# Later selection work for four head pairs and an earlier start of one feed-forward block, in a fused attention and MLP kernel on one Trainium2 core

## The chip, the cores and the metric

The kernel runs on one core of one Trainium2 chip. The metric is the device time of one execution in microseconds (us), and a smaller time is better. Each timed comparison runs both kernels in the same rounds on the same chip. "Span" is the length of one profiled execution, from the first to the last instruction; it is about 1.7 us shorter than the time of the same execution.

The engines of the core have short names in the profile: PE is TensorE (matrix multiplications), PEld its weight loads, DVE is VectorE, ACT is ScalarE, POOL is GpSimd, and SP is the sync engine, which here only starts DMA transfers (SPq is its queue). "L388" is line 388 of the kernel.

## The reference, cut to what matters

The model is an attention in which each query may only look at its six best chunks of keys, followed by a gated MLP with a spatial mixing matrix. There are 4 batch rows, 8 heads, 768 positions and 64 dimensions per head.

```python
def _attn_ref(q, k, v):                       # q, k, v: (4, 8, 768, 64)
    k_chunks = k.reshape(B, H, nc, 32, D)
    k_min, k_max = k_chunks.min(axis=3), k_chunks.max(axis=3)
    ub = np.sum(np.maximum(q[..., None, :] * k_min[:, :, None], q[..., None, :] * k_max[:, :, None]), -1)
    ub = np.where(causal, ub, -1e9)           # an upper bound for each query and chunk
    top_chunks = np.argsort(ub, axis=-1)[..., -6:]
    scores = scale * q @ k.transpose(0, 1, 3, 2)
    scores = np.where(sel & causal_mask, scores, -1e9)     # sel: the key's chunk is in top_chunks
    ...                                        # softmax
    return attn @ v

def _moe_ref(x, w_in, w_spatial, b_spatial, w_out):
    u, v = np.split(np.maximum(x @ w_in, 0.0), 2, axis=-1)
    v_n = (v - mean(v)) / sqrt(var(v) + 1e-6)
    v_s = einsum('ts,bsd->btd', w_spatial, v_n) + b_spatial[None, :, None]
    return (u * v_s) @ w_out
```

## The kernel before

The kernel works on 16 pairs of heads, four pairs to a batch row. It has one list of "beats", 12 to a pair; every piece of work is put at a beat, and the pieces are emitted in the order of beats. A beat is therefore not a time. It sets the order in which the pieces are handed over when the program is built, and so in the main the order of each engine's queue; each engine takes its queue in that order.

For each pair, the selection comes first: transpose the keys (`k_transpose`), reduce them to maxima and minima of chunks (`k_max`, `k_min`, two DVE reductions), transpose the queries, build the bounds, find the sixth best bound (`top`, MAX8 instructions) and write the not-chosen marks beside the queries (`select`). Then the queries with their marks are transposed to the operand `a` of the score matmuls. Pairs 0 to 7 do this on TensorE with a copy on ACT; pairs 8 to 15 do it by one DMA transpose from the sync engine.

```python
ps_sc  = ...psum_pool(bufs=3)     # scores
ps_tr  = ...psum_pool(bufs=1)     # ONE bank: q_transpose, bounds and a_transpose (pairs 4 and up)
ps_acc = ...psum_pool(bufs=1)     # ONE bank: attention output of a head
ps_ml  = ...psum_pool(bufs=3)     # feed-forward, transposed keys, weight transposes (and transposes of pairs 0-3)
qs_ring = [ring.tile(...) for i in range(3)]          # queries: three buffers of two pairs each

def a_transpose(self, hi):                            # [cut]
    if self.i >= 8:
        if hi == 0:
            nc.sync.dma_start_transpose(out=self.a..., in_=self.qs...)      # L246
        return
    self.tr = self.trans_tile()
    for t in range(NQT):
        nc.tensor.transpose(self.tr[...], self.qs[:, t, ...], identity)     # L251

# [cut] the loads: queries on the POOL queue, L336, and values, L343
for g in range(1, NPAIR // 2):                        # g: two pairs
    t0 = 2 * g * BEATS
    for hi in range(2):
        at(t0 - 40 + hi, load_k, g, hi)
        at(t0 - 36 + hi, load_q, g, hi)
    at(t0 - 18, load_v, g)
# [cut] scores, exponentials and values of pair i at beats 12 i to 12 i + 17
for i, p in enumerate(pairs):                         # the selection of pair i
    t0 = i * BEATS
    if i < 2:
        continue
    t0 += 4 if i < 4 else 0
    at(t0 - (22 if i < 4 else 27), p.k_transpose)
    at(t0 - 22, p.k_max)
    at(t0 - 21, p.q_transpose)
    at(t0 - 20, p.k_min)
    at(t0 - 19, p.q_parts, 0)
    at(t0 - 18, p.q_parts, 1)
    at(t0 - 17, p.k_bounds)
    at(t0 - 16, p.bounds)
    at(t0 - 15, p.k_operand, 0)
    at(t0 - 14, p.top, 0)
    at(t0 - 13, p.top, 1)
    at(t0 - 12, p.select)
    at(t0 - 11, p.k_operand, 1)
    at(t0 - 10, p.a_transpose, 0)
    at(t0 - 9, p.a_copy, 0)
    at(t0 - 7, p.a_transpose, 1)
    at(t0 - 6, p.a_copy, 1)
# [cut] feed-forward of batch row b: its matmuls are spread evenly over a stretch of beats
    first, count = (b + 1) * HP * BEATS + 13, HP * BEATS      # HP = 4 pairs to a row
    for cost, fn in steps:
        at(first + done * count // total, fn)
```

The softmax here doesn't subtract the row's maximum and nothing guards it: scores larger than these inputs give would overflow.

## Time and profile before

The time before was 208.66 us (median of 3 runs, 208.53 to 208.81).

| quantity, before | value | from |
|---|---|---|
| span | 206.9 us | the page |
| columns streamed by TensorE, at 2400 per us (213 ns for 512) | 171.6 us | all matmul records, added up |
| DVE busy in all | 154.5 us | the page |
| first feed-forward matmul | 55.09 us | the timeline |
| first scores of pair 9 | 97.1 us | the timeline |

The first part of the page of the kernel before says how busy each engine was: busy us, share of the span, number of instructions.

```profile
PE 187.8 (91%) x1922; PEld 115.1 (56%) x1922; DVE 154.5 (75%) x454; ACT 158.1 (76%) x326; POOL 80.5 (39%) x100
```

TensorE looks full at 91%, but 206.9 us minus 171.6 us of streamed columns leaves about 35 us in which it streamed nothing (33 us at the measured pace below). The Trainium skill ("Perfetto Trace Analysis", section "Identifying the Most-Contended Engine") says that matmul busy share is not a good measure of how close a kernel is to the limit, and this trace agrees. The measured pace is close to the 213 ns: at the end of the chain of waits (start, duration, what), 146 matmuls of 512 columns take 31.53 us back to back, 216 ns each.

```profile
171.50 31.53 PE mlp L388 x146
```

The table of stretches shows where that time lies. Its columns are the stretch, its length, then busy us and number of instructions (in brackets) of PE, PEld, DVE, ACT and POOL, then the granted TensorE clock, the DMA share and GB/s.

```profile
26.00:40.00 14.00, 12.94 (x195) 9.87 (x194) 12.61 (x41) 12.18 (x26) 10.15 (x15) 1.00 2.07 171
40.00:55.00 15.00, 12.85 (x195) 9.68 (x194) 12.90 (x37) 14.26 (x32) 12.28 (x14) 1.00 1.82 172
55.00:80.00 25.00, 24.39 (x294) 16.17 (x292) 23.72 (x79) 22.38 (x48) 15.72 (x18) 1.00 2.03 136
80.00:97.10 17.10, 17.10 (x193) 10.80 (x192) 15.72 (x48) 12.80 (x28) 6.48 (x7) 1.00 1.57 137
97.10:160.00 62.90, 62.90 (x629) 37.04 (x628) 50.25 (x150) 55.10 (x121) 12.17 (x14) 1.00 0.92 140
```

From 80 to 160 us TensorE is busy in every moment. From 26 to 55 us it isn't, while DVE is busy for 25.5 of 29 us and ACT for 26.4. That is the stretch that the change is about. The timeline of DVE before (start, duration, engine, line, operation, output<-input, count) shows how tightly the selection stands there: the two key reductions of pair 4 (L178, L182) stand around a part of the MAX8 instructions (L232) and ahead of the select (L237) of pair 3.

```profile
33.23 0.94 DVE L178 TENSOR_REDUCE kmm<-kTp 128x24 f16<-128x768 f16 x1
34.09 0.44 DVE L232 MAX8 max<-ub 128x8 f32<-128x20 f32 x4
34.45 0.94 DVE L182 TENSOR_REDUCE kmm<-kTp 128x24 f16<-128x768 f16 x1
35.30 0.40 DVE L237 TENSOR_TENSOR qs<-ub,max 128x240 f16<-128x240 f32 x1
```

And the timeline of all engines before, where pair 4 gets its first transposed operand:

```profile
41.31 0.40 DVE L237 TENSOR_TENSOR qs<-ub,max 128x240 f16<-128x240 f32 x1
...
42.20 0.50 PE L251 MATMUL tr<-identity,qs 128*128 128x128 f16 x6
...
42.98 0.82 ACT L257 COPY a<-tr 128x768 f16<-128x768 f16 x1
```

The select at 41.31 is pair 4's; 0.9 us later TensorE transposes for the operand `a` (L251), and ACT copies it at 42.98. In the timeline of ACT before, from 47.3 us on, stand pair 4's first exponentials:

```profile
47.12 1.39 ACT L271 ACTIVATE e<-sc 128x512 f16<-128x512 f32 x2
```

They began more than 3 us after this copy ended, so pair 4's selection had slack.

### The profile page before, as it was taken

To read this page: it belongs to the slowest core of one execution; us is meant where nothing else is said; L and a number is where in the kernel's file an instruction comes from. 1 tells how busy PE (TensorE), PEld (TensorE's weight loads), DVE (VectorE), ACT (ScalarE), POOL (GpSimd) and SP (SyncE) were. 2 spreads that over 40 slices of the span, in tenths; PEclk is the share of its full clock that TensorE was granted. 3 is DMA by queue.
4 is the path that set the end of the run, shared out by engine and by line. 5 is a ranking of instruction groups with operands and counts; after the bars stand their busy time and mean duration, and the time that the engine had idled before them with its cause. 6 is when DMAs were issued, how large, how long until landed. Compare 5 with 4: busy or idle time off the path is not lost.

```text
span 206.9 us, 5068 instructions
## 1 busy us (share of the span) xinstructions
PE 187.8 (91%) x1922; PEld 115.1 (56%) x1922; DVE 154.5 (75%) x454; ACT 158.1 (76%) x326; POOL 80.5 (39%) x100
## 2 busy tenths in 40 slices
PE   0368999898899999999999999999999999999992
PEld 0266776775666665656655656565555454444440
DVE  6467979989799989899797999887647456365520
ACT  4797989899998889785989996669999830666042
POOL 7997659596992463236114111111111110000000
PEclk9999999999999999999999999999999999999999
DMA  5999999999999999979998926648782124540356
GB/s 38 92 118 154 140 178 158 173 177 167 177 162 162 97 119 128 135 130 147 149 278 153 180 62 57 127 88 158 181 166 65 38 29 92 187 152 3 72 128 256
DMA packets 114424, 27.27 MB, mean 132 GB/s; under 512 B 109536, under 2 KB 110816, under 8 KB 114400
## 3 DMA queue, kind: packets, MB, share of 16 engines
q0 software_dynamic: 76544, 12.20, 89.8%
q1 hardware_dynamic: 37856, 14.75, 36.4%
q8 instruction: 15, 0.25, 0.5%
q14 instruction: 9, 0.07, 0.1%
HBM read 24.38 MB, written 6.29 MB: 148 GB/s over the span
## 4 chain that ended last, share of the span: by engine, by line
PE 69%; ACT 17%; DVE 8%; issue 2%; DMA 2%; POOL 0%; DVEq 0%; ACTq 0%; POOLq 0%
PE mlp L388 40%; PE sc L266 12%; ACT e L271 10%; PE acc L289 7%; PE kTp L170 2%; ACT a L257 2%; DVE kmm L178 2%; PE ub L222 2%; DMA k<-in_k_dram 2%; PE trm L251 2%; ACT vraw L398 1%; PE tr L205 1%; DVE vn L412 1%; DVE kmm L182 1%; ACT u L420 1%
## 5 line engine op out<-in xcount | busy, mean ns | idle before, releaser
L271 ACT ACTIVATE e<-sc 128x512 f16<-128x512 f32 x192 | 96.9, 553 | 14.8 <-PE sc L266 13.4
L266 PE MATMUL sc<-a,kh 128*128 128x512 f16 (+3 forms) x256 | 65.5, 308 | 2.1 <-ACT e L271 1.5
L388 PE MATMUL mlp<-w_in_sb,xT 128*128 128x512 f16 x192 | 53.0, 379 | 0.1
L278 POOL TENSOR_SCALAR_AFFINE_SELECT e<-e 128x768 f16<-128x768 f16 x24 | 20.9, 869 | 66.3 <-ACT e L271 66.3
L289 PEld LDWEIGHTS <-e 128*128 128x128 f16 x672 | 31.4, 97 | 17.0 <-DVE x L297 3.8
L388 PE MATMUL mlp<-vn,wsT 128*128 128x512 f16 x144 | 37.3, 379 | 0.0
L289 PE MATMUL acc<-vt,e 128*128 128x65 f16 x672 | 35.3, 193 | 0.7 <-DVE x L297 0.4
L266 PEld LDWEIGHTS <-kh 128*128 128x128 f16 x256 | 22.7, 98 | 13.3 <-issue 0.8
L437 ACT COPY o<-mlp 128x512 f32<-128x512 f32 x24 | 14.1, 586 | 19.5 <-PE mlp L388 19.1
L400 DVE BATCH_NORM_STATS2 stats<-vraw 128x6 f32<-128x512 f32 x24 | 16.6, 693 | 12.9 <-ACT vraw L398 12.5
L388 PE MATMUL mlp<-w_out_sb,gT 128*128 128x512 f16 x96 | 25.1, 379 | 0.0
L388 PEld LDWEIGHTS <-xT 128*128 128x128 f16 x192 | 17.2, 97 | 12.6 <-issue 0.4
L427 DVE SCALAR_TENSOR_TENSOR g<-mlp,b_col,u 128x512 f16<-128x512 f32 x24 | 17.9, 748 | 7.3 <-PE mlp L388 6.2
L232 DVE MAX8 max<-ub 128x8 f32<-128x8 f32 (+4 forms) x160 | 15.6, 165 | 5.1 <-PE ub L222 4.9
L388 PEld LDWEIGHTS <-wsT 128*128 128x128 f16 x144 | 12.9, 98 | 10.4
L178 DVE TENSOR_REDUCE kmm<-kTp 128x24 f16<-128x768 f16 x16 | 15.2, 948 | 3.7 <-PE kTp L170 2.7
L297 DVE TENSOR_TENSOR x<-acc,rec 128x384 f16<-128x384 f32 x32 | 17.6, 551 | 0.4
L336 POOL DMA_DIRECT2D qs<-in_q_dram x14 | 14.6, 1049 | 5.9 <-PE sc L266 5.9
L194 DVE COPY kh<-kTp 64x768 f16<-64x768 f16 x30 | 16.5, 549 | 0.5
L398 ACT ACTIVATE vraw<-mlp 128x512 f32<-128x512 f32 x24 | 14.4, 601 | 3.0 <-PE mlp L388 3.0
L420 ACT ACTIVATE u<-mlp 128x512 f16<-128x512 f32 x24 | 14.3, 598 | 1.7 <-PE mlp L388 1.5
L327 POOL DMA_DIRECT2D k<-in_k_dram x14 | 14.4, 1045 | 2.5 <-PE kTp L170 1.8
(67 smaller groups left out, 230.2 us busy)
## 6 DMA issues: line engine op xcount, KB each, us to landing
out_dram<-o SPq DMA_DIRECT2D x24, 256.0 KB, 2.3
vt<-in_v_dram POOLq DMA_DIRECT2D x8, 384.0 KB, 8.8
k<-in_k_dram POOLq DMA_DIRECT2D x14, 192.0 KB, 8.1
qs<-in_q_dram POOLq DMA_DIRECT2D x14, 192.0 KB, 7.5
ws_raw<-in_moe_w_spatial_dram POOLq DMA_DIRECT2D x6, 192.0 KB, 6.9
w_in_sb<-in_moe_w_in_dram POOLq DMA_DIRECT2D x8, 128.0 KB, 6.9
w_out_sb<-in_moe_w_out_dram POOLq DMA_DIRECT2D x4, 128.0 KB, 7.9
k<-in_k_dram POOLq DMA_DIRECT2D x4, 96.0 KB, 3.4
```

The source lines that it names most:

```text
L178: nc.vector.tensor_reduce(self.kmm[:, 0, :], self.kT.rearrange("d (c ch) -> d c ch", ch=CHUNK), axis=AX.X, op=Alu.max)
L194: copy(self.kh[hi][d0:d1], self.kT[d0:d1])
L266: mm(sc[:, col:col + n], lhsT=self.kh[hi][:, t * P:(t + 1) * P], rhs=self.a[:, q0 // P:(q0 + n) // P, hi, :], start=True, stop=not diag)
L271: nc.scalar.activation(out=self.e[hi][:, g * 512:g * 512 + width], in_=sc[:, 0:width], func=Act.Exp, scale=scale)
L278: nc.gpsimd.affine_select(out=blk, in_=blk, compare_op=Alu.is_ge, fill=0.0, base=0, channel_multiplier=-1, pattern=[[0, NQT], [1, P]])
L289: mm(self.av[:, qi, :], lhsT=self.e[hi][:, c:c + P], rhs=self.v[hi][:, t, 0:D + 1], start=first and n == 0, stop=last and n == len(blocks) ...
L297: nc.vector.tensor_tensor(self.x16[:, :, hi, :], in0=self.av[:, :, 0:D], in1=rec.to_broadcast([P, NQT, D]), op=Alu.mult)
L388: mm(st[group][:, 0:cols], lhsT=lhsT, rhs=rhs, start=(j == 0), stop=(j == n - 1))
L398: nc.scalar.activation(st["vraw"][:, ti, :], h, func=Act.Relu)
L400: nc.vector.bn_stats(stats, st["vraw"][:, ti, :])
L420: nc.scalar.activation(st["u"][:, ti, :], h, func=Act.Relu)
L427: nc.vector.scalar_tensor_tensor(g, in0=vs, scalar=b_col[:, ti:ti + 1], in1=st["u"][:, ti, :], op0=Alu.add, op1=Alu.mult)
```

## The change

The intent: selection work of pairs 4 to 7 was emitted earlier than needed and so competed with the pairs before it. It is put 8, 6, 4 and 2 beats nearer to its use; the key transposes of these pairs, which stood 5 beats ahead of their reductions, stand 1 beat ahead. The feed-forward of the first batch row begins 4 beats sooner, to put TensorE work where it had gaps. No work is added or removed.

```diff
         if i < 2:
             continue
-        t0 += 4 if i < 4 else 0
-        at(t0 - (22 if i < 4 else 27), p.k_transpose)
+        t0 += 4 if i < 4 else max(0, 8 - 2 * (i - 4))
+        at(t0 - (22 if i < 4 else 27 - 4 * (i < 8)), p.k_transpose)
         at(t0 - 22, p.k_max)
 ...
         first, count = (b + 1) * HP * BEATS + 13, HP * BEATS
+        if b == 0:
+            first, count = first - 4, count + 4
         total, done = sum(c for c, _ in steps), 0
```

## The prediction

> **What bounds the kernel now.** The page puts TensorE at 91% of the 206.9 us span, but the Trainium skill ("Perfetto Trace Analysis", section "Identifying the Most-Contended Engine") calls matmul busy % a poor measure of distance to roofline, as matmuls are pipelined. I count streamed columns instead. In the tail the chain of waits shows 146 matmuls of 512 columns in 31.53 us, 216 ns each: about 2.4 columns per ns. So the kernel holds about 171.6 us of columns. Time not covered by columns, per 10 us of the timeline: 9.3, 5.7, then 2.1, 2.8, 3.0, 1.8, 1.5, 1.0 from 20 to 80 us, then 0.3 to 0.4, which is back-to-back running. Three stages:
>
> 1. to about 15 us: loads and set-up;
> 2. 15 to 80 us: DVE, ACT and TensorE all nearly full (table of stretches, 26 to 97 us: DVE 64.95 of 71.1 us busy, ACT 61.62), no feed-forward before 55.1 us; ACT's exponentials and copies and DVE's selection set the pace;
> 3. from 80 us: TensorE alone.
>
> **What the change does.** No work added or removed. By the instruction order, the first difference is at pair 2's second head (about 30 us), and from pair 9 (scores from 97.1 us; 84 feed-forward matmuls issued in both) TensorE's order has the same counts again. So stage 3 is untouched; the gain or loss is how much earlier pair 9 starts.
>
> - Pair 4's two key reductions (0.86 us each, start to start) leave the DVE chain at 33.2-35.4 us, where they delay pair 3's select. Worth what ACT idles there, about 0.6 us.
> - 12 feed-forward matmuls (2.6 us) now stand before pair 5's scores, where none did, in a stretch (40-60 us) in which TensorE loses 4.8 us. Three ReLUs (0.5 us each) and two bound copies join ACT there, 2.0 us, so pair 5 starts not at 54.7 but about 56.5 us (estimate), with 33.2 instead of 29.9 us of columns done: 1.4 us net.
> - Cost: pair 4's first transposed operand is now made after pair 3's last scores, so transpose (0.34), ACT copy (0.8) and first score (0.43) stand in a row: an ACT bubble of about 1 us near 47 us.
> - From pair 5 to 9 the columns were 39.0 us in 42.5 us; smoother spreading may give 0.8 us.
>
> **Sum, an estimate:** 0.6 + 1.4 + 0.8 - 1.0, about 1.8 us. DVE's idle time from 26 to 97 us (6.1 us) caps the gain, its work there being unchanged.
>
> **Predicted:** 206.8 us, 80% range 205.1 to 208.6. Chances: faster by over 2% 0.06, within 2% 0.91, slower by over 2% 0.03.
>
> **What would show it right or wrong.**
> - Pair 9's scores start 1 to 3 us before 97.1 us; from there to the end unchanged (109.8 us) within 0.3 us.
> - First feed-forward matmul moves from 55.1 to 50-52 us.
> - Uncovered TensorE time from 40 to 80 us falls from 7.3 to about 5 us.
> - Pair 3's MAX8 and select finish 1 us or more earlier; DVE's total busy time stays (154.5 us).
> - A new ACT idle of 0.5 to 1.5 us before pair 4's first exponential.
>
> **What would make it wrong.** Selection so late that pairs 4 to 7 wait for it (DVE select, TensorE transpose, ACT copy, one PSUM buffer for transposes): TensorE's in-order queue stalls and 1 to 2 us are lost. The early feed-forward waiting for pair 3's transposed output or for weights. More gain, if the DVE contention at 33 to 46 us delayed more than ACT's visible idle time. A change of buffers that reaches the TensorE-bound stage.

## The result, and the profile after

The changed kernel took 212.06 us (median of 4 runs, 211.67 to 212.41), against 208.74 us (208.53 to 209.19) for the kernel before in the same rounds. The ratio is 1.0158, with a 95% interval of 1.0138 to 1.0178. Ratios here are the mean time of one kernel's runs over the mean of the other's runs of the same rounds, so not quite the ratio of the medians quoted. Executions over 1.5% slower than the fastest of the same kernel are left out of the means. The kernel got slower by 3.3 us; a gain of about 1.8 us had been predicted.

The first part of the page of the kernel after:

```profile
PE 189.7 (90%) x1922; PEld 116.3 (55%) x1922; DVE 155.3 (74%) x454; ACT 157.7 (75%) x326; POOL 80.7 (38%) x100
```

No work was added: the instruction counts are the same. The tail is the same too, in the chain of waits after:

```profile
175.28 31.53 PE mlp L388 x146
```

The table of stretches after, for the same stretches:

```profile
26.00:40.00 14.00, 12.82 (x186) 9.78 (x185) 10.60 (x31) 12.91 (x28) 10.13 (x15) 1.00 2.08 172
40.00:55.00 15.00, 12.35 (x175) 9.17 (x174) 12.99 (x44) 10.53 (x25) 12.54 (x15) 0.89 1.80 170
55.00:80.00 25.00, 24.01 (x295) 16.32 (x295) 23.34 (x68) 23.27 (x50) 12.85 (x15) 1.00 1.62 113
80.00:97.10 17.10, 17.10 (x197) 10.90 (x196) 16.67 (x54) 13.31 (x30) 7.08 (x8) 1.00 1.73 142
97.10:160.00 62.90, 61.60 (x622) 36.17 (x620) 49.84 (x152) 52.52 (x114) 13.51 (x15) 1.00 1.03 145
```

DVE's idle time from 26 to 40 us rose from 1.39 to 3.40 us (14 us minus the busy time). From 40 to 55 us ACT lost 3.7 us of work. And in the last stretch, where TensorE had been busy throughout, 1.3 us are missing.

To place the loss, the streamed columns are a better ruler than wall time. For each kernel I added up the columns of its matmuls in order of start, divided by 2400 per us (which is 512 in 213 ns), and read off the time at which fixed amounts had been reached. The difference from before is the delay at the same amount of work done:

| columns done, us | 20 | 40 | 60 | 75 | 80 | 170 |
|---|---|---|---|---|---|---|
| time before, us | 39.82 | 65.50 | 87.38 | 102.85 | 107.94 | 201.12 |
| delay of after, us | -0.13 | +2.23 | +2.28 | +2.54 | +3.93 | +3.78 |

There are two losses: about 2.3 us between 40 and 65 us (the early loss), and 1.4 us at about 110 us (the late loss). From 40 to 75 us of columns, and after 80, the delay in this table changes by 0.3 us at most. In finer steps, the early loss is mainly one stall: at 24 us of columns (44.6 us of its own time) after is 0.67 us ahead, at 26 (50.5 us) it is 2.58 us behind, a loss of 3.25 us, of which 1.2 us is won back by 30 and most of that lost again by 40.

**The early loss.** The DVE timeline after:

```profile
34.08 0.37 DVE L237 TENSOR_TENSOR qs<-ub,max 128x240 f16<-128x240 f32 x1
...
37.78 0.96 DVE L178 TENSOR_REDUCE kmm<-kTp 128x24 f16<-128x768 f16 x1 [0.98 <-PE kTp L170]
...
38.76 0.92 DVE L182 TENSOR_REDUCE kmm<-kTp 128x24 f16<-128x768 f16 x1
```

Pair 3's select came 1.2 us earlier, as wanted (34.08 against 35.30). But the first key reduction of pair 4 now starts at 37.78 instead of 33.23, and DVE sat idle for 0.98 us before it, waiting for the key transposes (kTp) of TensorE. The timeline of all engines after, where pair 4 gets its operand. The bracket at the end of a line is the idle time of that engine before it and what ended it:

```profile
45.02 0.40 DVE L237 TENSOR_TENSOR qs<-ub,max 128x240 f16<-128x240 f32 x1
...
45.47 0.44 PE L205 MATMUL tr<-identity,qs 128*128 128x128 f16 x5 [0.56 <-DVE qs L237]
...
46.66 0.55 DVE L297 TENSOR_TENSOR x<-acc,rec 128x384 f16<-128x384 f32 x1
...
47.27 0.54 PE L289 MATMUL acc<-vt,e 128*128 128x65 f16 x12 [1.36 <-DVE x L297]
...
47.66 0.51 PE L251 MATMUL tr<-identity,qs 128*128 128x128 f16 x6
...
48.21 0.80 ACT L257 COPY a<-tr 128x768 f16<-128x768 f16 x1 [1.36 <-PE tr L251]
...
49.06 1.01 PE L266 MATMUL sc<-a,kh 128*128 128x512 f16 x2 [0.60 <-ACT a L257]
...
49.68 0.60 ACT L271 ACTIVATE e<-sc 128x512 f16<-128x512 f32 x1 [0.67 <-PE sc L266]
```

Pair 4's select is done at 45.42 (before 41.71). TensorE's next instruction is pair 5's query transpose, which waits for the bank that this select frees (45.47). Then TensorE stands 1.36 us for DVE's normalisation of the output (L297), which stands behind other selection work in DVE's queue. Only then does it make pair 4's operand, ACT copies it (48.21), and the scores wait for ACT. Pair 4's first exponential is at 49.68, before 47.12. ACT's idle times from 44 to 50 us, two of them before lines not shown here, add up to 0.71 + 1.10 + 1.36 + 0.67 = 3.84 us.

The chain of waits says the same in short. From 44 to 52 us exponentials on ACT make 70.8% of it before. After, it runs from 43.90 to 47.22 us through DVE, with both key reductions of pair 5 (L178, L182) around pair 4's select:

```profile
44.24 0.86 DVE kmm L178
45.10 0.31 DVE qs L237
45.41 0.86 DVE kmm L182
```

**The late loss.** The chain of waits after, around 100 us:

```profile
96.16 5.49 DMA xT<-x
101.65 8.81 DMA a<-qs
...
110.51 0.39 PE sc L266
```

A DMA is the longest piece of it: the operand transpose of pair 10 took 8.81 us from issue to landing, and TensorE waited for it. (The piece above it ends where this transpose is issued.) To see why, here is first the POOL timeline of before, with the query loads (L336) and the value load (L343):

```profile
91.38 2.04 POOL L336 DMA_DIRECT2D qs<-in_q_dram  x2 [3.21 <-PE sc L266]
...
94.23 1.43 POOL L343 DMA_DIRECT2D vt<-in_v_dram  x1
```

And the POOL timeline of after:

```profile
93.54 1.43 POOL L343 DMA_DIRECT2D vt<-in_v_dram  x1 [2.62 <-PE sc L266]
...
96.79 2.04 POOL L336 DMA_DIRECT2D qs<-in_q_dram  x2 [0.94 <-DMA a<-qs]
```

The last query loads fill the buffer that pair 9's operand transpose has read, so they wait for that transpose (`DMA a<-qs`). It was issued at 86.90 before and 91.40 after. The loads go out at 96.79 instead of 91.38, behind the value load instead of ahead of it, and so they run beside the operand transpose of pair 10. (The beats of these loads are the same in both kernels, 126 for the value load and 132 and 133 for the query loads, yet their order on POOL differs. So the beat alone does not fix it; no run isolates what does.) The timeline of the sync queue before, with the transposes of pairs 9 and 10:

```profile
86.90 1.44 SPq L246 DMA_TRANSPOSE a<-qs  x1
...
99.30 3.35 SPq L246 DMA_TRANSPOSE a<-qs  x1
```

And of the sync queue after:

```profile
91.40 1.44 SPq L246 DMA_TRANSPOSE a<-qs  x1
...
101.65 4.42 SPq L246 DMA_TRANSPOSE a<-qs  x1
```

The transpose was issued 2.35 us later, landed 8.81 us after issue instead of 7.07, and pair 10's first exponential began at 111.00 instead of 107.07. The 7.07 us of before are long too: there the value load, issued at 94.23 and landing 9.2 us later, ran beside the transpose, but TensorE did not have to wait for it.

### The profile page after: what moved, and what is told of

It is laid out like the page before. It is cut to its first block, busy times and chain, and to the rows that moved or that the text cites. A ratio compares the mean times of both kernels' runs of the same rounds, so it can differ in the third digit from the quotient of the medians.

```text
span 210.7 us, 5070 instructions
## 1 busy us (share of the span) xinstructions
PE 189.7 (90%) x1922; PEld 116.3 (55%) x1922; DVE 155.3 (74%) x454; ACT 157.7 (75%) x326; POOL 80.7 (38%) x100
## 4 chain that ended last, share of the span: by engine, by line
PE 64%; ACT 18%; DMA 8%; DVE 6%; issue 2%; POOL 0%; ACTq 0%; DVEq 0%; POOLq 0%
PE mlp L388 37%; PE sc L266 11%; ACT e L271 10%; PE acc L289 6%; DMA a<-qs 4%; ACT a L257 3%; DMA xT<-x 3%; ACT vraw L398 2%; PE kTp L170 2%; DMA k<-in_k_dram 2%; PE ub L222 1%; PE trm L251 1%; DVE vn L412 1%; DVE kmm L178 1%; PE tr L251 1%
## 5 line engine op out<-in xcount | busy, mean ns | idle before, releaser
L271 ACT ACTIVATE e<-sc 128x512 f16<-128x512 f32 x192 | 95.8, 554 | 16.8 <-PE sc L266 15.6
L266 PE MATMUL sc<-a,kh 128*128 128x512 f16 (+3 forms) x256 | 66.2, 314 | 3.2 <-DMA a<-qs 1.2
L388 PE MATMUL mlp<-w_in_sb,xT 128*128 128x512 f16 x192 | 53.8, 379 | 0.3
L289 PE MATMUL acc<-vt,e 128*128 128x65 f16 x672 | 35.8, 194 | 1.8 <-DVE x L297 1.6
L266 PEld LDWEIGHTS <-kh 128*128 128x128 f16 x256 | 23.2, 99 | 15.9 <-DMA a<-qs 1.7
L178 DVE TENSOR_REDUCE kmm<-kTp 128x24 f16<-128x768 f16 x16 | 15.1, 944 | 4.4 <-PE kTp L170 3.4
L297 DVE TENSOR_TENSOR x<-acc,rec 128x384 f16<-128x384 f32 x32 | 17.6, 550 | 0.3
L343 POOL DMA_DIRECT2D vt<-in_v_dram x8 | 11.5, 1440 | 13.7 <-PE sc L266 11.4
L336 POOL DMA_DIRECT2D qs<-in_q_dram x14 | 14.6, 1051 | 2.8 <-PE tr L251 1.5
```

What stands on the lines that cost most here:

```text
L178: nc.vector.tensor_reduce(self.kmm[:, 0, :], self.kT.rearrange("d (c ch) -> d c ch", ch=CHUNK), axis=AX.X, op=Alu.max)
L266: mm(sc[:, col:col + n], lhsT=self.kh[hi][:, t * P:(t + 1) * P], rhs=self.a[:, q0 // P:(q0 + n) // P, hi, :], start=True, stop=not diag)
L271: nc.scalar.activation(out=self.e[hi][:, g * 512:g * 512 + width], in_=sc[:, 0:width], func=Act.Exp, scale=scale)
L289: mm(self.av[:, qi, :], lhsT=self.e[hi][:, c:c + P], rhs=self.v[hi][:, t, 0:D + 1], start=first and n == 0, stop=last and n == len(blocks) ...
L297: nc.vector.tensor_tensor(self.x16[:, :, hi, :], in0=self.av[:, :, 0:D], in1=rec.to_broadcast([P, NQT, D]), op=Alu.mult)
L388: mm(st[group][:, 0:cols], lhsT=lhsT, rhs=rhs, start=(j == 0), stop=(j == n - 1))
```

## The experiments

Eighteen kernels ran. The rival theories at the start, by the letters that some expectations use: S, the swap stalls TensorE in pairs 4 to 7; F, the earlier feed-forward crowds the scores; L, the selection is simply too late for its use; and for the late loss, that the last query loads collide with an operand transpose. D came later: DVE work put off from 26 to 40 us falls due where DVE has no room. The rounds ran on different chips, so kernels of different rounds are compared by their ratios to before; a difference of two such ratios is uncertain by about 0.6 us either way, by the 95% intervals. Each time is a median with the median of the kernel before in the same rounds. "Delay" is the delay against before in the table above.

### 1. Each half of the change alone

Only the feed-forward lines:

```diff
 # against before
+        if b == 0:
+            first, count = first - 4, count + 4
```

> Only the earlier feed-forward. Theory S (swap: since each pair's shift is two beats smaller than the one before it, pair i+1's query transposes now stand ahead of pair i's operand transposes in TensorE's queue and in the one transpose bank, and pair 4's scores wait for that) and theory L (lateness: the selection is simply emitted too near to its use) both expect no loss here: 208.0 to 209.0 us, ratio 0.997 to 1.002. Theory F (the earlier feed-forward crowds ACT and DVE before pair 5) expects most of the loss here: 210.5 us or more.

Measured: 209.77 against 208.72 us, ratio 1.0051 (1.0020 to 1.0082). The delay is -0.01 us at 40 us of columns, +0.19 at 75 and +0.87 at 80. So the earlier feed-forward alone causes no early loss, but no early gain either: its first matmul moved from 55.09 to 53.98 us and nothing came of it. Its loss is mainly the late one. The list of waits of this run (engine, line, releaser, us in total, times, longest) has the wait that the run of before doesn't have:

```profile
PE sc L266 <- DMA a<-qs: 0.5, 1, 0.5
```

Only the selection lines:

```diff
 # against before
-        t0 += 4 if i < 4 else 0
-        at(t0 - (22 if i < 4 else 27), p.k_transpose)
+        t0 += 4 if i < 4 else max(0, 8 - 2 * (i - 4))
+        at(t0 - (22 if i < 4 else 27 - 4 * (i < 8)), p.k_transpose)
```

> Only the later selection. S and L expect the whole loss or nearly so: 211 to 213 us, ratio 1.012 to 1.020, with pair 4's first exponential near 49.7 us as in the changed kernel. F expects 209 us or less.

Measured: 212.44 against 208.72 us, ratio 1.0185 (1.0144 to 1.0226). The delay is +3.75 us at 40 and only 0.3 us more at 80. The early loss therefore comes from the selection shift, and the feed-forward, put on top of it, wins back about 1.5 us early in the profiled runs (after stands at +2.28 where this kernel stands at +3.78, at 60) and loses it late; by the ratios after is 0.6 us faster. Theory F is out.

### 2. The swap

The query transposes of pairs 5 to 8 two beats later, which puts them back behind the operand transposes:

```diff
 # against after
-        at(t0 - 21, p.q_transpose)
+        at(t0 - 21 + 2 * (5 <= i <= 8), p.q_transpose)
```

> The changed kernel with the query transposes of pairs 5 to 8 two beats later, so that each stands again behind the operand transposes of the pair before (seen in the instruction order); nothing else is edited. S expects pair 4's first exponential back at 46.5 to 48 us (49.7 in the changed kernel) and 208 to 210 us. L expects no help: 211.5 to 213 us, as the operand is made at the same beat. If the second loss (pair 10's operand by DMA, 8.8 us to landing) is independent of the first, about 1.5 us of loss stays: 209.5 to 210.5 us.

Measured: 212.16 against 208.72 us, ratio 1.0157 (1.0130 to 1.0183). That is exactly the loss of the full change. The mechanism did move. In the timeline of ACT in this run, pair 4's operand copy is at 45.76 (after 48.21) and its first exponential at 47.36 (after 49.68):

```profile
45.76 0.80 ACT L257 COPY a<-tr 128x768 f16<-128x768 f16 x1 [0.73 <-PE tr L251]
...
47.36 1.08 ACT L271 ACTIVATE e<-sc 128x512 f16<-128x512 f32 x2 [0.29 <-PE sc L266]
```

But the time was lost again. At 40 the delay is +1.47, at 75 it is +3.94. A new wait came up, in the list of waits of this run:

```profile
PE acc L289 <- POOL e L278: 1.9, 2, 1.6
```

Pair 4 started 2.3 us earlier and the total didn't change: between 24 and 26 us of columns this kernel loses 1.26 us, where after loses 3.25, but it loses more later. So the swap lengthens the stall at pair 4, and still theory S, the swap as the cause of the slowdown, falls.

### 3. Other shifts

Half the shift, with steps of one beat; the full shift with steps of one beat; and the shift without pair 4:

```diff
 # three kernels, each against after
-        t0 += 4 if i < 4 else max(0, 8 - 2 * (i - 4))
+        t0 += 4 if i < 4 else max(0, 4 - (i - 4))                      # e4_half_shift
+        t0 += 4 if i < 4 else max(0, 8 - (i - 4))                      # e5_full_no_swap
+        t0 += 4 if i < 4 else max(0, 8 - 2 * (i - 4)) * (i > 4)        # e6_pair4_early
```

> The changed kernel with shifts 4, 3, 2, 1 instead of 8, 6, 4, 2 for pairs 4 to 7 (no swap either, by the instruction order). Theory L (the later the selection, the more TensorE waits for it) expects about half of the selection's loss, with pair 4's select at 43 us (41.3 before, 45.0 changed): 210.0 to 211.0 us. A rival, T (threshold: any shift that breaks the old interleaving loses all of it), expects 211.5 us or more; a third, N (a small shift is free, as the select was 4 us ahead of need), expects 208.5 to 209.5 us.

> The changed kernel with shifts 8, 7, 6, ... 1 for pairs 4 to 11 instead of 8, 6, 4, 2 for pairs 4 to 7: pair 4 as late as in the change, the later pairs later still, but the step is one beat, and the instruction order shows no swap. S expects 208 to 210 us and pair 4's first exponential at 46.5 to 48 us; L expects at least the loss of the change, 212 us or more.

> The changed kernel with pair 4 alone at its old beats; pairs 5, 6, 7 still 6, 4, 2 later, with the swap among them. If the loss is made at the boundary of pairs 3 and 4, as the waits at 45 to 49 us say, the delay after 25 us of columns falls from 1.6 us to under 0.3 and the whole to 209.5 to 210.5 us. If pairs 5 to 7 lose by themselves, 211 us or more.

Measured, ratio to before: 1.0161 (1.0104 to 1.0217) at 211.60 us for the half shift; 1.0200 (1.0170 to 1.0230) at 212.87 us for the full shift in steps of one; 1.0212 (1.0189 to 1.0235) at 213.06 us with pair 4 left early. The half shift varied (211.09 to 213.86), and its profile fell on its slowest run, which has a TensorE wait of 2.82 us for pair 9's operand: that transpose took 9.07 us to landing, beside the value load (92.95 us, landing 9.8 us later) and before any of the last query loads was issued. Nothing finer is read from it. No amount of shift helped, with or without the swap, and leaving pair 4 where it was is not a remedy (its delay is +2.01 at 40): pair 4's late start is not the whole of the early loss. All three still have the short distance of the key transposes, which experiment 4 takes up.

### 4. The distance of the key transposes

The old distance of 5 beats between key transposes and their reductions, with all the rest of the change:

```diff
 # against after
-        at(t0 - (22 if i < 4 else 27 - 4 * (i < 8)), p.k_transpose)
+        at(t0 - (22 if i < 4 else 27), p.k_transpose)
```

> The changed kernel with the old distance of 27 beats for the key transposes of pairs 4 to 7 (the change made it 23). Theory L expects no difference from the changed kernel, 211.5 to 212.5 us. If the key reductions on DVE are late because their transposes come just before them (a wait of 0.98 us at 37.8 us in the changed kernel), 1 us comes back: 210.5 to 211.2 us.

Measured: 210.93 against 208.68 us, ratio 1.0104 (1.0082 to 1.0126). About 1.1 us of the 3.3 came back (0.0054 of 208.7). The delay is +1.35 at 40 instead of +2.23. This difference is there before the stall at pair 4: at 20 us of columns this kernel is 1.05 us ahead of before, where after is 0.13 ahead. The stall itself stays: from 24 to 26 us of columns it costs 2.97 us here (3.25 in after). The DVE timeline of this run shows the wait gone:

```profile
35.15 0.94 DVE L178 TENSOR_REDUCE kmm<-kTp 128x24 f16<-128x768 f16 x1
...
37.20 0.92 DVE L182 TENSOR_REDUCE kmm<-kTp 128x24 f16<-128x768 f16 x1
```

Pair 4's first key reduction starts at 35.15 directly after the work before it; after, it started at 37.78, after 0.98 us of waiting for TensorE. With one beat of distance the transposes stand behind more matmuls in TensorE's queue, and they are not done when DVE gets to them.

### 5. The last query loads

Two kernels without the last query loads (pairs 14 and 15), which give a wrong result; e8 is the full change, e11 the feed-forward alone:

```diff
-            at(t0 - 36 + hi, load_q, g, hi)
+            if g < 7:
+                at(t0 - 36 + hi, load_q, g, hi)
```

> Wrong result on purpose: the changed kernel without the last two query loads (pairs 14 and 15 read old queries). They are the loads issued at 96.8 and 97.8 us, just before pair 10's operand transpose, which then took 8.8 us to land. If they are what delays it, it lands in under 7 us, TensorE's wait of 1.4 us at 110.5 us is gone and the time is 210.3 to 211.0 us. If the value load of 93.5 us or the transposes ahead of it in its queue delay it, the wait stays: 211.5 us or more.

> Wrong result on purpose: the kernel with only the earlier feed-forward, without the last two query loads. If the wait of 0.7 us for pair 10's operand at 107.5 us is all that the earlier feed-forward costs, and these loads cause it, the time is that of the kernel before, 208.4 to 209.0 us, ratio 0.998 to 1.002. If the feed-forward costs by crowding the engines, 209.4 us or more stays.

Measured: e8 took 211.29 against 208.68 us, ratio 1.0120 (1.0101 to 1.0139), so 0.8 us came back; the time is 0.3 us above the range expected. e11 took 208.58 against 208.57 us, ratio 0.9998 (0.9983 to 1.0013): the loss of the earlier feed-forward is gone entirely. Both also move less data, so by themselves they can't tell the collision from the bytes. The next one can: a fourth query buffer, with which the last loads need not wait for pair 9's operand and go out long before, with the same bytes and a correct result.

```diff
 # against after
-    qs_ring = [ring.tile(...) for i in range(3)]
+    qs_ring = [ring.tile(...) for i in range(4)]        # and "% 3" becomes "% 4" in both uses
+    at(B0, init_ring, 3)
```

> The changed kernel with four query buffers instead of three, so that the last two query loads need not wait for pair 9's operand transpose and go out before it (right result). If those loads in the wrong place cause the DMA wait, it falls under 0.3 us and the time to 210.3 to 211.2 us; the early loss of 2.3 us by 40 us of columns stays. If not, 211.5 to 212.5 us.

Measured: 211.36 against 208.57 us, ratio 1.0132 (1.0114 to 1.0150); the time is 0.2 us above the range expected. The delay stays at +2.54 from 75 to 80, where after gained another 1.39. The list of waits of this run has no TensorE wait for an operand DMA at all. Its sync queue shows the operand transpose of pair 10:

```profile
101.84 1.27 SPq L246 DMA_TRANSPOSE a<-qs  x1
```

It is issued at 101.84, as late as in after (101.65), but takes the sync engine 1.27 us instead of 4.42. The view of tile `a` from 96 to 118 us gives the landing times of two such transposes (pairs 10 and 11), first for after:

```profile
DMA to landing us min/median/max: 5.2/7.0/8.8
```

And the same view of this run:

```profile
DMA to landing us min/median/max: 3.7/4.1/4.6
```

Pair 10's is the longest in after, 8.81 us, and the shortest here: 3.68 us. In e11 it is 3.70. So the cause of the late loss is shown: it is the query loads beside the operand transpose. (Its size is less certain, see the end of this section. And other ordinary loads lengthen a transpose too, as the value load did in before and in the half shift.) The Trainium skill ("DMA: Bandwidth & Descriptors", section "Issuing engines are not separate DMA queues") says that DMAs from all issuing engines end on the same 16 DMA engines and interleave there. The trace agrees: the loads were issued by POOL and the transpose by the sync engine, and the latter took 5.1 us longer.

### 6. Half shifts at the old distance, with and without the rest

```diff
 # e10: before, with this line alone; e13: this line, the feed-forward lines and four query buffers
-        t0 += 4 if i < 4 else 0
+        t0 += 4 if i < 4 else max(0, 4 - (i - 4))
```

> The kernel before with shifts of 4, 3, 2, 1 beats for pairs 4 to 7 and nothing else. In the half-shift run with the earlier feed-forward the first 40 us of columns came 0.3 us late at most, and the loss was a wait for a DMA transpose at 101.5 us. If that wait belongs to the earlier feed-forward, this run loses nothing: 208.0 to 209.3 us and no DMA wait over 0.3 us on TensorE. If the selection shift alone makes it, 210 us or more.

> The half shift, the earlier feed-forward and four query buffers together. If early waits grow only beyond the half shift and the late wait is the misplaced query loads, both losses are gone: 208.0 to 209.5 us, and perhaps a little under the kernel before. If the loads are not the cause, the wait of the half-shift run stays: 211 us or more.

Measured: e10 took 210.83 against 208.57 us, ratio 1.0109 (1.0092 to 1.0126); e13 took 210.74, ratio 1.0100 (1.0083 to 1.0117). In e10 the delay is +0.55 at 40 and +2.44 at 60, in e13 +0.51 and +2.25: with a smaller shift, a loss of similar size comes, but later; whether it is of the same kind was not found out. e10 has none of the causes found so far (no swap, the old key distance, no TensorE wait for an operand DMA) and loses 2.3 us all the same. The hoped-for version that beats both kernels wasn't found here.

### 7. Selection earlier than before

```diff
 # against before
-        t0 += 4 if i < 4 else 0
+        t0 += 4 if i < 4 else -2 * (i < 8)
```

> The kernel before with the selection of pairs 4 to 7 two beats EARLIER, nothing else. Theory D (DVE: its work up to pair 9 is the same in every version, 55.5 to 56.2 us between 10 and 60 us of columns, and any selection work put off leaves DVE idle early and falls due when it has no room) expects no loss, 207.5 to 209.0 us. A rival, O (the old order is simply tuned to the beat and any move breaks it), expects 210 us or more, as with the half shift the other way (210.8).

Measured: 210.46 against 208.92 us, ratio 1.0073 (1.0048 to 1.0097). Moving the selection of pairs 4 to 7 the other way loses too, where theory D had expected no loss. "Later is worse" is not a law here; the interleave of before was better than each one tried on either side of it.

### 8. Relief and load for DVE

Theory D says that DVE is short of time where the put-off work falls due. Then relief should help and load should hurt. For relief, half of the spatial weight copies went from DVE to ACT, in the changed kernel (e15) and in the kernel before (e16, the control):

```diff
-        nc.vector.tensor_copy(wsT[:, so, :], tr)
+        (nc.scalar.copy if so % 2 else nc.vector.tensor_copy)(wsT[:, so, :], tr)
```

> The changed kernel with three of the six copies of the transposed spatial weights on ACT instead of DVE (about 0.5 us each taken off DVE at 60 to 80 us, 0.8 us each put on ACT). D expects a gain, 0.7 to 1.5 us: 210.5 to 211.3 us. If the loss is made by waits in the queues and not by DVE's load, no gain: 211.7 to 213 us.

> The same three copies on ACT in the kernel before, as the control: D expects less than in the changed kernel, from 0.7 us faster to 0.5 us slower, 208.0 to 209.2 us.

Measured: e15 took 213.23 against 208.92 us, ratio 1.0201 (1.0181 to 1.0222; one slow run of 217.74 us is left out); e16 took 209.11, ratio 1.0007 (0.9989 to 1.0025). Moving 1.6 us of DVE work to ACT (where it takes 2.5 us) is free in the kernel before and costs about 0.9 us in the changed one. Both expected ranges for e15 are missed. But it is no test of relief where the early loss arises: the three copies ran at 67.3, 73.2 and 79.9 us, after the stall at pair 4, and the delay at 40 us of columns is unchanged (+2.26 against +2.23).

For load, two more key reductions, of pairs 6 and 7, into a scratch tile that nobody reads (1.8 us in all):

```diff
 # against after, in k_max
+            if self.i in (6, 7):
+                twice = sb.tile([P, NCH], F16, tag="twice", name="twice")
+                nc.vector.tensor_reduce(twice, self.kT..., axis=AX.X, op=Alu.max)
```

> The changed kernel with the first key reduction of pairs 6 and 7 done twice (0.86 us of DVE each, start to start, at about 50 and 60 us; the copy is not used). D expects nearly the whole 1.7 us to show: 213.0 to 214.5 us. If DVE has room there, under 0.6 us: 212.0 to 212.7 us.

Measured: 214.50 against 208.92 us, ratio 1.0271 (1.0244 to 1.0298). That is 0.0113 more than the full change, or 2.4 us for 1.8 us of work. The two ran at 49.3 and 60.6 us, and the delay at 40 us of columns is +4.68: DVE time in this stretch does reach the total. So load fits theory D, as does the chain of waits through DVE; e15 shows only that more ACT work from 67 us on costs time in the changed kernel. Relief of DVE between 40 and 50 us was not run, and e14 contradicts D's forecast, so D stays unproven.

### 9. The found causes removed together

e18 is the full change with the old key distance (experiment 4) and four query buffers (experiment 5). e19 is e18 with the swap undone as well (experiment 2).

> The changed kernel with the old distance of the key transposes and with four query buffers: both repairs that helped alone (210.9 and 211.4 us). If they add up, the DMA wait is gone and 1.4 us of early loss stays: 209.8 to 210.5 us. If they overlap, 210.6 to 211.2 us.

> The same with the swap of the transposes undone as well, so that only the lateness itself is left of the selection part. If the swap costs once the other two are gone, 208.8 to 209.7 us; if the lateness alone makes the rest (undoing the swap gave nothing before), within 0.4 us of the run with the swap, 209.8 to 210.8 us.

Measured: 209.99 against 208.84 us for both, ratios 1.0046 (1.0022 to 1.0070) and 1.0044 (1.0023 to 1.0066). Of the excess of 0.0158, removing the two causes together takes away 0.0112, or 2.3 us. This is no budget of independent causes: e10 has neither and loses as much. Undoing the swap changes nothing in the total, for the second time, within 0.7 us.

This pair also bears on a suspicion about the clock. TensorE ran at half clock for 3.41 us in the changed kernel (from 49.0 us; the 0.89 in the table of stretches after). The Trainium skill ("TensorE: Matmul & The Clock Gate", section "What's actually happening") states that the clock falls to half after an idle window of about 3.4 us. The length of the slow stretch agrees with that window, but TensorE was not idle before it: it was busy for 1.52 us of the 3.41. From 40 to 55 us e18 has the clock at 0.89 and e19 at 1.00, with equal total times, and the same holds for after at 0.89 and e3 at 1.00; e19's four timed runs all have a mean clock of 1.000. So the throttle is not needed for the loss. That it costs nothing is not shown, since both pairs also differ by the swap. Six kernels have timed runs of both kinds, with a mean clock of 0.988 to 0.992 and of 0.996 to 1.000; the former took 0.4 us longer on average (from 0.1 us less in e7 to 0.7 us more in e18, with one to three runs of each kind).

| kernel | delay at 20 | 40 | 60 | 75 | 80 | 170 |
|---|---|---|---|---|---|---|
| after | -0.13 | +2.23 | +2.28 | +2.54 | +3.93 | +3.78 |
| e1, feed-forward alone | -0.08 | -0.01 | +0.18 | +0.19 | +0.87 | +0.71 |
| e2, selection alone | -0.60 | +3.75 | +3.78 | +3.77 | +4.01 | +3.84 |
| e3, swap undone | -0.37 | +1.47 | +2.96 | +3.94 | +3.94 | +3.77 |
| e7, old key distance | -1.05 | +1.35 | +1.39 | +1.39 | +1.89 | +1.75 |
| e12, four query buffers | -0.24 | +2.33 | +2.53 | +2.54 | +2.54 | +2.38 |
| e18, both | -0.88 | +1.67 | +1.87 | +1.88 | +1.88 | +1.72 |
| e19, both, swap undone | -0.86 | +0.18 | +0.98 | +1.66 | +1.66 | +1.49 |

The profiled run of after puts the late loss at 1.4 us, those of e1 and e7 at 0.7 and 0.5. The timed ratios put it at 0.5 us (after against e12) and 1.2 us (e7 against e18), each within 0.6 or 0.7 us. Its size is not settled; the profiled run of after, its slowest, shows it large.

## Why the prediction was wrong

It said 206.8 us (205.1 to 208.6), and 212.06 us were measured. Two steps failed: the sum for the stretch up to pair 9, where pair 9's scores were to start about 1.8 us earlier and started 2.3 us later (99.4 against 97.1), and the claim that nothing changes from there on, where 1.5 us were lost. Point by point:

- **"Three stages", "stage 3 is untouched".** This step failed, and its cause is shown. From pair 9 TensorE has the same instructions in the same order, which the prediction had checked, and it took for granted that the time would be the same, 109.8 us. It was 111.3 us. The order of one engine doesn't fix when the DMAs of others meet. Pair 9's select came at 90.9 instead of 86.3 us, and that moved the last query loads beside pair 10's operand transpose (e8, e11 and e12). The prediction named "a change of buffers that reaches the TensorE-bound stage" as a risk; it was a buffer's release time, with no buffer changed.
- **"An ACT bubble of about 1 us near 47 us".** This is the term of the sum that was mis-sized most. The place was right, the size was not: 3.84 us of ACT idle time, pair 4 started 2.56 us late, and 3.25 us were lost between 24 and 26 us of columns. The prediction added up transpose, copy and first score in a row, as if DVE and TensorE were free when these came. They weren't: TensorE stood for the bank and for DVE's normalisation first. The prediction's own list of what would make it wrong describes this stall well. Yet shortening the stall of pair 4 (e3) bought nothing in the total, so the full cause lies deeper than this one stall.
- **"Pair 4's two key reductions leave the DVE chain … worth about 0.6 us".** Pair 3's select did finish 1.2 us earlier and its first exponential came at 38.45 instead of 39.81 us. The gain was real: with the old key distance the kernel is 1.05 us ahead at 20 us of columns (e7). In the change itself 0.13 us of it was left, and the stall at pair 4 took more than that back. What the prediction left out is the other side of it: the chain of waits at pair 4 now runs through the DVE work that was put off. DVE idled 2.0 us more from 26 to 40 us, about half of that before the reduction which waited for the key transposes.
- **The key transposes.** The prediction gave no term to the change of their distance from 5 beats to 1. It was worth 1.1 us alone (e7 against after) and 1.8 us with the late loss out of the way (e18 against e12), each within 0.6 us.
- **"1.4 us net" for feed-forward before pair 5.** Alone it gained nothing (e1, -0.01 us at 40): this fits a stretch that TensorE doesn't pace, so that filling its gaps earlier doesn't end it earlier. 12 feed-forward matmuls did stand before pair 5, as foretold, but pair 5's first exponential came at 60.11 us, not at 56.5. On top of the selection shift the feed-forward used gaps that this shift had made, about 1.5 us in the profiled runs.
- **"Smoother spreading may give 0.8 us".** No gain of this kind was seen. The TensorE time not covered by streamed columns from 40 to 80 us rose from 7.3 to 9.3 us; it was predicted to fall to 5.
- **Right:** no work was added (same instruction counts, DVE 155.3 against 154.5 us), the first feed-forward matmul moved to 52.75 us (predicted 50 to 52, so just outside), and the tail stayed.

**What stays open.** About 1.0 us (ratio 1.0046) remains with both causes removed. More than that arises between 20 and 60 us of columns: e18 goes from 0.88 us ahead to 1.87 behind, 2.75 us, where after goes from 0.13 ahead to 2.28 behind, 2.41 us. So restoring the key distance gave the kernel its early lead back and left this loss as it was. The loss belongs to the shift of the selection itself, since e1 doesn't have it. Its cause is not settled: the swap isn't it in the total (e19), the clock isn't it (e19), and of theory D only the load side was tested where the loss arises (e17). That every other placement tried also lost, earlier ones (e14) and half ones (e10), suggests but doesn't show that before's interleave was tuned to this stretch as a whole. Four buffers in the kernel before were not run.

No version that ran beat the kernel before. e16 equals it, and so does e11, with a wrong result.

## What to carry to other kernels

Emitting work "nearer to its use" need not be a gain in a stretch where two engines are nearly full: ask where the put-off work will find a free place, and let a producer (here the key transposes) keep its lead over the consumer on another engine. When an engine's instruction order is unchanged in a stage, ask also when buffers come free before it and which DMAs that starts, since a load that goes out 5 us later may run beside a transfer that somebody waits for. And before a stall seen in the profile is called the cause, take it away alone: here the start of a pair was brought forward by 2.3 us and the total stayed the same.

## What the Trainium skill lacked or had wrong

- "DMA: Bandwidth & Descriptors": its table "Latency and other measured facts" gives a DMA transpose with a non-contiguous middle dimension an effective 261 GB/s. An estimate from that rate alone for this operand (128 partitions of 1536 fp16 values, 393 kB) is 1.5 us. Measured from issue to landing, it was 3.68 us with no loads beside it (e12) and 8.81 us with the query loads (7.07 in the kernel before, with the value load). The 3.68 us do not show the rate to be wrong, since a rate leaves out any fixed cost. I found no figure there for a transpose beside ordinary loads.
- The same page, section "Issuing engines are not separate DMA queues", calls the sequencer's time to initiate a DMA "usually small relative to the DMA itself". For this transpose the sync engine's record lasted 1.27 of 3.68 us, and 4.42 of 8.81 us when the query loads ran beside it, which is half.
- "TensorE: Matmul & The Clock Gate": it speaks of an idle window, but I found no figure there for how much work in the window still counts as idle. TensorE was not idle here: in the eight profiled runs with a fall it had been busy for 1.49 to 1.63 of the 3.41 us before it. The amount alone does not decide: in the profiled run of e2 a stretch of 3.41 us (45.17 to 48.58) had only 1.44 us of work, and its clock stayed whole.
- I found no page that says how to judge, from a static instruction order, what a moved piece of work is worth when two engines are both nearly full. The runs show that the sum of local gains had the wrong sign: +1.8 us predicted, -3.3 us measured.
